# A second PSUM bank for every other head pair's weighted sums in the first batch, with a redrawn order of work

## The chip, the cores and the metric

The kernel runs on one core of a Trainium2 chip. The metric is the device time of one execution in microseconds (us). The core has five engines that run side by side: TensorE (PE, matrix products, with its weight loads PEld), VectorE (DVE), ScalarE (ACT), GpSimd (POOL) and SyncE (SP, which here only issues DMAs). Results of matrix products go to PSUM, an accumulator memory of eight banks.

## What is computed

Attention over the best key chunks, followed by a two-layer MLP with an ELU between its layers. There are 4 batches, 8 heads, 768 positions and 64 dimensions per head. For every query, an upper bound of its score with each chunk of 32 keys is worked out from the minimum and maximum of the chunk's keys; the six best chunks are kept.

```python
ub = np.sum(np.maximum(q[:, :, :, None, :] * k_min[:, :, None, :, :],
                       q[:, :, :, None, :] * k_max[:, :, None, :, :]), axis=-1)
ub = np.where(causal, ub, -1000000000.0)
top_chunks = np.argsort(ub, axis=-1)[..., -top_k:]
...
scores = np.where(mask, scores, -1000000000.0)
attn = np.exp(scores - np.max(scores, axis=-1, keepdims=True))
attn = attn / (np.sum(attn, axis=-1, keepdims=True) + 1e-09)
x = np.matmul(attn, v)            # then heads side by side: 3072 x 512
h = x @ w_in                      # 512 x 2048
g = np.where(h > 0.0, h, np.exp(np.minimum(h, 0.0)) - 1.0)
out = g @ w_out                   # 2048 x 512
```

## The kernel before

**Tiles and stages.** The queries are cut into nine blocks. Batch 0 has three blocks of 256 positions (blocks 0, 1 and 2), every later batch two of 384. Heads go in pairs, four pairs (j = 0 to 3) to a block. For each block i:

- *loads*: k, q and v of 128 positions at a time (L463), into buffers kld, qld and vld. Block 0's k and q are loaded by SP and ACT, most of blocks 1 and 2 by POOL's queue. The weights w_in (L480) and w_out (L484) come as four pieces each on POOL's queue. `SW_ORDER` fixes the order in that queue: k1, v0, q1, v1, the four pieces of w_in, k2, q2, v2, the four of w_out.
- *prep_k, prep_q*: PE transposes k and q (L501) into PSUM; VectorE takes chunk maxima and minima (L521), ScalarE copies out (L528, L533, L548, L553), VectorE makes the positive part of q (L564).
- *select*: PE works out the bounds (L586), VectorE transposes them (L597), takes the best eight (L604), compares (L608) and transposes the masks back (L614 for blocks 0 to 2).
- *score*: PE makes the scores of a pair (L649, with a causal mask added by L652 in blocks 0 and 1), ScalarE the exponentials into pt (L668).
- *weigh*: PE makes the weighted sums and, in a 65th column per head, the sum of the weights (L703). VectorE takes the reciprocal (L712) and multiplies (L714) into the tile on. In the first and the last block PE transposes on (L722) and VectorE copies it into xt (L725); elsewhere a DMA transposes it (L727).
- *mlp*: h = x @ w_in on PE (L744), the exponential on ScalarE (L748), a step on POOL (L750), maximum and minimum on VectorE (L752), then g @ w_out on PE (L765), a copy on ScalarE (L769) and the store (L772).

**PSUM.** Seven banks form the shared pool psM, from which transposes, bounds, scores and MLP tiles are taken in turn. The eighth is a single fixed tile, `o_bank`: the weighted sums of every head pair go to its columns 0 to 389 (0 to 259 are used by a block of 256). Its columns 400 to 511 take filler matmuls.

**The order of work.** The program does not run its stages one after the other. Every step is handed to a planner (`Plan.op`) with its engine, an assumed time, what it reads and writes, and a priority. The priority is the slot of its block plus an offset from the table `SHIFTS`, which has one number for each kind of step, engine and block. `Plan.run` then plays the engines forward: of the steps whose operands and buffers are ready it takes the one that can start first, and of two that can start at the same time the one with the lower priority number. `EARLY` is the time up to which it assumes shorter latencies: 1100 ns rather than `DMA_END` = 1500 from a DMA's end of transfer to its landing, and 50 rather than `MARGIN` = 80 ns for a dependency between engines. The order that comes out is the program's order on each engine; on the chip each engine follows it strictly and waits on semaphores.

**Fillers.** Where the plan leaves PE idle for longer than about 600 ns before 70 us, the program puts matmuls on constant data into the gap (L886), and 30 of them at the start. They write `o_bank`, and so are ordered against VectorE's reading of that bank.

```python
o_bank = psum["psO"].tile([P, 512], F32, name="o_bank")
...
o3 = Buf("psO", lambda: o_bank[:, 0:6 * (D + 1)].rearrange("p (h q d) -> p h q d", h=2, q=3))
...
            if o.start < FILL_END:
                for _ in range(int((o.start - pe - 100) / FILL_NS) if pe else FILL_FIRST):
                    nc.tensor.matmul(o_bank[:, 400:512], lhsT=junk, rhs=junk[:, 0:112], start=True, stop=True)
```

## Time and profile before

| what | value |
|---|---|
| median of six runs | 290.72 us (289.49 to 292.06) |
| the profiled execution | 292.06 us, of which 290.3 us from the first to the last instruction (the span) |
| granted PE clock, mean | 0.986 |
| PE in the span | 275.7 us busy |
| matmuls of the output layer (L765) | 384, 99.6 us busy |
| matmuls of the input layer (L744) | 576, 93.2 us |
| scores (L649) | 312, 59.5 us |
| weighted sums (L703) | 672, 29.6 us |
| fillers (L886) | 43, 5.6 us |
| reciprocals (L712) | 36, 152 to 197 ns each |
| normalisations (L714) | 36, 414 to 558 ns each |
| DMA | 36.22 MB, mean 125 GB/s |

Times run from the start of the span. A line such as L703 is a line of the code above. A row of the timeline gives the start, the length from the first start to the last end, the engine, the line, the operation, what it writes and reads, and how many instructions it merges; in brackets stands how long the engine was idle before it and what ended the wait. Rows can overlap, since matmuls are pipelined. A row of the waits gives who waited for whom, the total in us, how many times, and the longest. The rows of busy tenths cut the span into 40 slices. A row of a table of windows gives the stretch, its length, the busy time of PE, PEld, DVE, ACT and POOL, then the granted clock of PE, the DMA share and GB/s.

### The profile page before, as it was taken

What the parts mean: (1) busy time and instruction counts of PE and PEld (TensorE: products, weight loads), DVE (VectorE), ACT (ScalarE), POOL (GpSimd) and SP (SyncE); (2) the same over time, 40 slices, a digit from 0 to 9 for tenths busy, and PEclk for the clock granted to TensorE, in tenths of its full rate; (3) what the DMA queues carried; (4) which work ended last, traced back from release to release, by engine and by line L of the source; (5) the groups of instructions that cost most, each with busy time, mean ns of one, the idle gap of its engine ahead of it and who ended that gap; (6) DMA issues with size and microseconds to landing.
All of it is one profiled execution on the core that took longest, in us unless ns stands there. A gap on an engine that the chain in (4) does not pass through costs nothing.

```text
span 290.3 us, 7076 instructions
## 1 busy us (share of the span) xinstructions
PE 275.7 (95%) x2519; PEld 179.0 (62%) x2519; DVE 191.5 (66%) x608; ACT 195.2 (67%) x434; POOL 130.5 (45%) x256
## 2 busy tenths in 40 slices
PE   7786989999999999999999999999999999999993
PEld 6474766688587566766646556656765556655541
DVE  8855887957869967759677966623598757525420
ACT  2895565698366799876855548868875397675530
POOL 8669771039167005852158615631581134204600
PEclk9998979999999999999999999999999999999999
DMA  8899997557956223985269526951212310010031
GB/s 188 228 229 205 290 187 120 128 152 163 213 129 159 58 61 73 256 215 129 47 167 248 136 54 152 232 154 55 65 27 66 88 55 3 0 66 8 0 111 73
DMA packets 86883, 36.22 MB, mean 125 GB/s; under 512 B 74176, under 2 KB 82880, under 8 KB 86848
## 3 DMA queue, kind: packets, MB, share of 16 engines
q1 hardware_dynamic: 79424, 27.38, 39.7%
q0 software_dynamic: 5344, 7.87, 13.3%
q10 hardware_dynamic: 2080, 0.52, 0.8%
q8 instruction: 20, 0.33, 0.5%
q14 instruction: 15, 0.12, 0.2%
HBM read 27.26 MB, written 6.29 MB: 116 GB/s over the span
## 4 chain that ended last, share of the span: by engine, by line
PE 75%; DVE 10%; DMA 7%; ACT 4%; SPq 2%; issue 1%; POOL 0%; ACTq 0%; POOLq 0%
PE psM L765 25%; PE psM L744 23%; PE psM L649 11%; PE o_bank L703 6%; PE psM L501 6%; DMA qld<-in_q_dram 3%; PE psM L586 3%; SPq L463 2%; DVE rhs L614 2%; DMA kld<-in_k_dram 2%; DVE gT L752 2%; DMA xt<-on 1%; DVE kmx L521 1%; ACT pt L668 1%; DVE kst L521 1%
## 5 line engine op out<-in xcount | busy, mean ns | idle before, releaser
L750 POOL TENSOR_SCALAR e<-e 128x384 f32<-128x384 f32 (+1 forms) x120 | 63.4, 535 | 89.7 <-ACT e L748 63.9
L765 PE MATMUL psM<-w_out_sb,gT 128*128 128x512 bf16 x384 | 99.6, 379 | 0.0
L668 ACT ACTIVATE pt<-psM 128x384 bf16<-128x384 f32 (+1 forms) x168 | 81.3, 562 | 18.8 <-PE psM L649 17.0
L744 PE MATMUL psM<-xt,w_in_sb 128*128 128x384 bf16 (+1 forms) x576 | 93.2, 311 | 0.6 <-DMA xt<-on 0.6
L752 DVE SCALAR_TENSOR_TENSOR gT<-psM,e 128x384 bf16<-128x384 f32 (+1 forms) x120 | 67.5, 580 | 32.6 <-POOL e L750 25.7
L748 ACT ACTIVATE e<-psM 128x384 f32<-128x384 f32 (+1 forms) x120 | 62.5, 532 | 30.2 <-PE psM L744 28.1
L744 PEld LDWEIGHTS <-w_in_sb 128*128 128x128 bf16 x576 | 55.9, 99 | 29.3 <-issue 2.4
L649 PE MATMUL psM<-rhs,lhs 96*128 96x256 bf16 (+2 forms) x312 | 59.5, 286 | 0.4 <-DVE rhs L614 0.3
L765 PEld LDWEIGHTS <-gT 128*128 128x128 bf16 x384 | 36.0, 97 | 30.6 <-DVE gT L752 0.6
L561 POOL TENSOR_SCALAR rhs<-QTf 64x384 bf16<-64x384 f32 (+1 forms) x56 | 28.6, 510 | 43.5 <-ACT QTf L548 40.1
L649 PEld LDWEIGHTS <-lhs 96*128 96x128 bf16 x312 | 29.3, 100 | 16.9 <-DVE rhs L614 0.6
L703 PEld LDWEIGHTS <-pt 128*128 128x128 bf16 x672 | 27.0, 98 | 8.5 <-issue 1.8
L769 ACT ACTIVATE osb<-psM 128x512 f32<-128x512 f32 x24 | 14.4, 606 | 23.9 <-PE psM L765 15.2
L703 PE MATMUL o_bank<-vext,pt 128*128 128x65 bf16 x672 | 29.6, 194 | 0.2
L521 DVE TENSOR_REDUCE kmx<-psM 128x12 f32<-128x384 f32 (+1 forms) x36 | 17.7, 505 | 9.4 <-PE psM L501 9.2
L548 ACT ACTIVATE QTf<-psM 128x384 f32<-128x384 f32 (+1 forms) x36 | 15.3, 470 | 10.8 <-PE psM L501 10.6
L492 POOL TENSOR_SCALAR vext<-vld 128x384 bf16<-128x384 f32 (+1 forms) x36 | 16.6, 480 | 9.5 <-DMA vld<-in_v_dram 8.6
L681 DVE TENSOR_TENSOR pt<-pt,tri 128x512 bf16<-128x512 bf16 x28 | 12.2, 436 | 11.8 <-ACT pt L668 11.7
L501 PE MATMUL psM<-ident_f,kld 128*128 128x128 f32 x96 | 17.2, 306 | 2.2 <-ACT rhs L553 0.6
L714 DVE TENSOR_TENSOR on<-o_bank,rcp 128x384 bf16<-128x384 f32 (+1 forms) x36 | 18.3, 507 | 0.8
L501 PE MATMUL psM<-ident_f,qld 128*128 128x128 f32 x96 | 16.8, 308 | 2.0 <-ACT rhs L553 0.8
L533 ACT ACTIVATE kb<-psM 128x384 bf16<-128x384 f32 (+1 forms) x28 | 14.1, 504 | 5.9 <-DVE kst L521 4.6
(56 smaller groups left out, 208.9 us busy)
## 6 DMA issues: line engine op xcount, KB each, us to landing
out_dram<-osb SPq DMA_DIRECT2D x24, 256.0 KB, 2.3
kld<-in_k_dram SPq DMA_DIRECT2D x19, 256.0 KB, 4.0
qld<-in_q_dram SPq DMA_DIRECT2D x19, 256.0 KB, 3.5
vld<-in_v_dram SPq DMA_DIRECT2D x18, 256.0 KB, 4.0
lhs<-kb SPq DMA_DIRECT2D x48, 48.0 KB, 1.9
w_in_sb<-in_moe_w_in_dram POOLq DMA_DIRECT2D x4, 512.0 KB, 10.3
w_out_sb<-in_moe_w_out_dram POOLq DMA_DIRECT2D x4, 512.0 KB, 9.4
vld<-in_v_dram POOLq DMA_DIRECT2D x6, 256.0 KB, 5.6
```

Source lines behind the costliest of these rows:

```text
L501: nc.tensor.transpose(ps.get()[:, P * n:P * (n + 1)], xb.get()[:, n, hs, :].rearrange("p h d -> p (h d)"), ident_f)
L521: nc.vector.tensor_reduce(out=out, in_=psk.get()[:, 0:w].rearrange("p (c w) -> p c w", w=CHUNK), axis=AX.X, op=o)
L561: pool_op(110 + pool_ns(w), lambda h=h: nc.gpsimd.tensor_scalar(out=rhs[RH[i]][0:64, h, j, 0:w], in0=qtf.get()[64 * h:64 * h + 64, 0:w], s ...
L649: nc.tensor.matmul(sps.get()[:, o + pc:o + pc + n], lhsT=lhs[s][0:96, hd, P * kb:P * (kb + 1)], rhs=rhs[y][0:96, hd, j, c0 - lo:c0 - lo + ...
L668: op("ACT", act_ns(wtot), 140, lambda pt=pt, sps=sps, hd=hd, wtot=wtot: nc.scalar.activation(out=pt.get()[:, hd, 0:wtot], in_=sps.get()[:, ...
L703: nc.tensor.matmul(o3.get()[:, hd, qi, :], lhsT=pt.get()[:, hd, P * qt + off:P * qt + off + P], rhs=vexts[s][:, kb, hd, :], start=(kb == 0 ...
L714: op("DVE", dve_ns(w), 140, lambda: nc.vector.tensor_tensor(out=on.get()[:, 0:nt, :, :].rearrange("p q h d -> p h q d"), in0=o3.get()[:, : ...
L744: op("PE", 1 + w / 2.4, 200, lambda fc=fc, kk=kk, h_ps=h_ps, o=w * (fc - f0): nc.tensor.matmul(h_ps.get()[:, o:o + w], lhsT=w_in_sb[:, kk, ...
L748: op("ACT", act_ns(m * w), 200, lambda e=e, h_ps=h_ps: nc.scalar.activation(out=e.get()[:, 0:m * w], in_=h_ps.get()[:, 0:m * w], func=AF.E ...
L750: op("POOL", pool_ns(m * w), 72, lambda e=e: nc.gpsimd.tensor_scalar(out=e.get()[:, 0:m * w], in0=e.get()[:, 0:m * w], scalar1=-1.0, scala ...
L752: g = op("DVE", dve_ns(m * w), 130, lambda e=e, h_ps=h_ps, f0=f0: nc.vector.scalar_tensor_tensor(out=gT[f0 // 4].get()[:, f0 % 4:f0 % 4 + ...
L765: op("PE", 216, 200, lambda tt=tt, fc=fc, o_ps=o_ps: nc.tensor.matmul(o_ps.get(), lhsT=gT[fc // 4].get()[:, fc % 4, P * tt:P * (tt + 1)], ...
```

## The change

In blocks 0, 1 and 2 (`O_TWO = 3`), the pairs j = 1 and j = 3 take their weighted sums to a tile from the pool psM; pairs 0 and 2, and all pairs of later blocks, keep `o_bank`. The reciprocal and the normalisation read the tile that was chosen. The number of psM banks stays at seven.

Three assumptions of the planner change: `EARLY` goes from 30 to 16 us, the early DMA latency from 1100 to 800 ns, the early margin from 50 to 40 ns. The whole table `SHIFTS` has new numbers, so that the order on every engine can differ over the whole run. The rows below are the ones that the prediction speaks of; the other rows change in the same way.

```diff
+O_TWO = 3
...
-EARLY = 30e3
+EARLY = 16e3
...
-    ('mlp_in', 'PE'): (2.58869, 0.18485, -0.03717, -4.42605, -1.68403, 0.1887, -0.63691, 0.32029, -2.51407),
+    ('mlp_in', 'PE'): (-2.53111, -2.44679, -2.98032, 0.33104, -2.87733, -0.07855, -1.6966, 0.41874, 6.39981),
...
-    ('mlp_out', 'PE'): (0.24075, 0.17459, 0.14942, -0.16027, 6.11871, 0.1171, 7.22562, 0.28947, -0.95423),
+    ('mlp_out', 'PE'): (-10.79, 2.66429, 7.78478, 3.00852, 0.48571, -0.12355, 2.30605, -1.71352, 7.21788),
...
-    ('score', 'PE'): (0.62726, 0.20683, -0.02773, 0.15303, -0.32678, -2.74631, 0.19235, -0.05167, 0.25745),
+    ('score', 'PE'): (2.99497, 0.39571, 0.05518, 0.69914, -0.09628, -9.67742, -0.07612, -6.04773, -0.26933),
...
-    ('select', 'PE'): (-3.8939, -8.46886, -9.81244, -9.94423, -3.54113, -5.76916, -5.21074, -7.35482, -7.76008),
+    ('select', 'PE'): (5.7063, -2.31403, 0.4375, -3.43262, -4.63267, 2.70558, -0.49943, 0.70776, -0.72468),
...
-    ('weigh', 'PE'): (8.24559, -1.30337, -3.1578, -2.868, -0.84271, -0.35438, -0.13752, 4.33018, -0.6965),
+    ('weigh', 'PE'): (0.16623, -7.89219, -11.11109, -10.94577, -20.56845, -12.32231, -16.82659, -6.87226, -5.74106),
...
-                done.end = clock + (1100 if clock < EARLY else DMA_END)
+                done.end = clock + (800 if clock < EARLY else DMA_END)
...
-                o.end = t + o.occ + o.lat + (50 if t < EARLY else MARGIN)
+                o.end = t + o.occ + o.lat + (40 if t < EARLY else MARGIN)
...
-        o3 = Buf("psO", lambda: o_bank[:, 0:6 * (D + 1)].rearrange("p (h q d) -> p h q d", h=2, q=3))
+        ob = buf("psM", [P, 512], F32) if j % 2 and i < O_TWO else Buf("psO", lambda: o_bank)
+
+        def o3():
+            return ob.get()[:, 0:6 * (D + 1)].rearrange("p (h q d) -> p h q d", h=2, q=3)
...
-                nc.tensor.matmul(o3.get()[:, hd, qi, :], lhsT=pt.get()[:, hd, P * qt + off:P * qt + off + P],
+                nc.tensor.matmul(o3()[:, hd, qi, :], lhsT=pt.get()[:, hd, P * qt + off:P * qt + off + P],
                                  rhs=vexts[s][:, kb, hd, :], start=(kb == 0), stop=(kb == qt))
...
-        op("DVE", 100, 120, lambda: nc.vector.reciprocal(out=rcp.get()[:, :, 0:nt], in_=o3.get()[:, :, 0:nt, D:D + 1]),
-           reads=[o3], writes=[rcp])
+        op("DVE", 100, 120, lambda: nc.vector.reciprocal(out=rcp.get()[:, :, 0:nt], in_=o3()[:, :, 0:nt, D:D + 1]),
+           reads=[ob], writes=[rcp])
```

## Prediction

> **What bounds the kernel now.** I read the page's engine rows first, then the waits of PE, then the timeline of PE over the head, and last tables of windows there.
>
> ```profile
> PE 275.7 (95%) x2519; PEld 179.0 (62%) x2519; DVE 191.5 (66%) x608; ACT 195.2 (67%) x434; POOL 130.5 (45%) x256
> PE   7786989999999999999999999999999999999993
> ...
> PE o_bank L886 <- DVE on L714: 3.0, 4, 0.8
> ```
>
> PE is the bound: 14.6 us of the span are not PE. Of these about 1.1 lie before the first instruction, 4.7 after the last matmul (285.57 of 290.3), 7.4 between 4 and 40 us, and only about 1.4 anywhere between 40 and 285 us. So an order of work can gain next to nothing after 40 us; it can lose there. The largest single wait of PE is a filler matmul (L886) that waits for VectorE's normalisation L714 to let go of the output bank: 4 times 0.75 us. The timeline of PE shows where:
>
> ```profile
> 20.86 0.22 PE L703 MATMUL o_bank<-vext,pt 128*128 128x65 bf16 x2
> 21.82 0.21 PE L886 MATMUL o_bank<-junk 128*128 128x112 bf16 x1 [0.73 <-DVE on L714]
> 21.87 0.27 PE L722 MATMUL psM<-ident_b,on 128*128 128x128 bf16 x2
> 21.98 0.34 PE L703 MATMUL o_bank<-vext,pt 128*128 128x65 bf16 x6
> 23.07 0.21 PE L886 MATMUL o_bank<-junk 128*128 128x112 bf16 x1 [0.75 <-DVE on L714]
> 23.12 0.27 PE L722 MATMUL psM<-ident_b,on 128*128 128x128 bf16 x2
> 23.23 0.35 PE L703 MATMUL o_bank<-vext,pt 128*128 128x65 bf16 x6
> ```
>
> Reader: this is block 0, one head pair after another: weighted sum (L703), VectorE, transposes (L722), next pair. One pair takes 1.25 us (21.82 to 23.07), and PE works about 0.5 of it. It goes on until 25.79, where the first MLP (L744) begins. The third view, busy time in windows of 3.4 us, shows a second price:
>
> ```profile
> 22.90:26.30 3.40, 1.72 (x26) 1.33 (x26) 2.10 (x9) 2.28 (x8) 3.40 (x6) 1.00 1.24 206
> 26.30:29.70 3.40, 3.40 (x22) 2.08 (x29) 1.35 (x5) 1.04 (x2) 3.09 (x4) 0.50 1.25 209
> ...
> 36.50:39.90 3.40, 2.24 (x15) 1.21 (x13) 3.28 (x9) 2.34 (x7) 2.49 (x6) 1.00 1.21 195
> 39.90:43.30 3.40, 3.39 (x28) 3.02 (x29) 2.84 (x7) 2.28 (x7) 3.00 (x8) 0.51 1.19 177
> ```
>
> The columns are length, busy PE, PEld, DVE, ACT, POOL, then the granted clock. After a window with 1.72 us of PE work, the next ran at 0.50; after one with 2.24 us, again 0.51. Each such stretch costs 3.4 x 0.5 = 1.7 us of full-speed work. The six runs support that size: 289.49, 289.93, 289.97 in one group and 291.47, 291.61, 292.06 in another, 1.9 us apart, about one stretch. The profiled execution is the 292.06 one, span 290.3 and 1.76 around it.
>
> **What the Trainium skill says.** "TensorE: Matmul & The Clock Gate", section "What's actually happening": PE's clock is halved after a window of about 3.4 us that was too idle and restored after a busy one, and the window runs freely. The two stretches agree in length (3.4 us); the place of the window against the program I take as a matter of luck. "PSUM — Partial Sum Buffer", section "PSUM bank collisions raise a hardware error": two engines must be kept apart by bank, not by address. The trace agrees: the filler writes columns 400 to 511, the normalisation reads columns up to 259, and the filler still waits 0.75 us. "PSUM", section "Engine vs sequencer instructions": matmuls start in program order. So everything behind a waiting matmul waits too; the transposes after each filler show it.
>
> **The change, part by part.**
> *The bank.* In blocks 0 to 2, pairs 1 and 3 write their weighted sums to one of the seven psM banks. In block 0 the sums of pair j+1 can then run while VectorE normalises pair j. What is late next is VectorE itself: its reciprocal 0.10 (busy after overlap, 0.17 as listed), normalisation 0.43, copy L725 0.29, gaps of 0.02 to 0.04, so about 0.85 per pair in place of 1.25. Four pairs: 4 x 0.40 = 1.6 us. In the blocks 1 and 2, PE has scores and MLP between the sums (41 to 60 us, idle 0.1 us): gain 0.
> *Pool pressure.* Each of the six pairs holds one of seven psM banks from the first sum to the end of the normalisation, about 0.9 us (0.3 + 0.55). Six times 0.9 over 7 banks is 0.8 us at most if the pool were what PE waits for. The waits of PE after 45 us name no bank (only two DMAs, 0.6 and 0.5), so I take 0, with 0.8 as the upper end; a gain below nothing is excluded, since the pool does not grow.
> *The new priorities.* Each number of SHIFTS moves a group of one engine and block in the planner's order, with no new work. For block 0 the sums on PE go from 8.25 to 0.17, the scores from 0.63 to 2.99: sums used to come behind the scores of all four pairs, and now come as soon as a pair's exponentials are there. VectorE sat idle 2.18 us before 21.12, so the chain can start earlier, up to 1.5 us (first sums near 19.5 in place of 20.46 to 20.9, masks of L614 end at 18.9). But two things hold the end. ScalarE finishes its last exponential of block 0 at about 21.8; with sums 0.3, reciprocal and normalisation 0.55, transposes 0.2 and copy 0.3 that gives 23.2. And w_in: its four loads issue at 16.5 to 18.7 on POOL and land 7.6 to 13.0 us later, so not before 24.1; v of block 1 and the casts of v of block 0 stand ahead of them in the same queue. So the MLP of block 0 starts at 24.1 at best, 25.79 now: 1.7 us for bank and order together, which I take (bounds: 0.7, if only half the overlap is planned; 1.7).
> *What follows.* The select of block 1 (L586 at 29.4) heads a VectorE chain from 30.7 to 38 that holds PE at 34.8 and 39.2 (0.31 and 0.65 us; a third wait, 0.45 at 37.6, is for ScalarE). It moves up with the MLP. It could move further: its q is copied by 24.6, so L586 could run near 25.5 rather than 29.4. Value between 0 and about 2 us (the 1.4 us of stalls and 0.6 of filler time); I take 0.3.
> *The clock.* A denser 20 to 26 us may spare the first stretch, and a different 36 to 40 us the second: 0 to 3.4 us in the profiled execution, minus 1.7 if a new one appears. The median of before already holds half of one such event. I take half a stretch, 0.85 us, less the slack below.
> *Planner constants.* EARLY from 30 to 16 us, 1100 to 800 and 50 to 40: these are times that the planner assumes, no instruction changes. For 16 to 30 us it now assumes later DMA landings, so PE is handed fewer operands too soon. Taken at 0; bounds are the stalls of the head.
> *After 40 us.* 1.4 us of idle PE can only shrink by that; a redrawn order of 56 loads and 28 transposes on SP's queue can open new waits like the 0.62 us one for xt at 145.9. Taken at +0.3, bounds -1 and +4.
>
> Sum: -1.7 - 0.3 - 0.85 + 0.3 = -2.55 us. Against the profiled 292.06 this gives 289.5; the median lies 1.34 lower because half of its runs show the cheaper head, so 290.72 - 2.55 = 288.2 us.
>
> **Rivals.**
> *A, the forecast*, 288.2 us, own range 286.6 to 289.2.
> *B, the whole head is repacked.* For it: all 7.4 us of idle and 3.4 us of half clock lie before 44 us, and VectorE is idle from 18.9 to 21.1 and from 27.4 to 29.4. Against it: DMA is full from 16 to 46 us (shares above 1). Bank and order 1.7, both stretches 3.4 less the half event (0.85) in the median, stalls of select 1.2: 290.72 - 5.45 = 285.3 us.
> *C, hidden.* The gain of block 0 is swallowed at the next gate (w_in, or VectorE's masks of block 1, which pin 34.8 us): 0.7 left, spent on one new wait of about 0.6 us: 290.6, range 289.3 to 292.1.
> *D, slower: PE stands before w_out.* The out-MLP of block 0 goes from 0.24 to -10.79 on PE, so it comes first as soon as the planner thinks w_out is in SBUF. On the chip w_out is issued at 30.5 to 36.2 and lands 7.7 to 13.1 us later, 38.2 to 49.3; before, its first matmul runs at 44.8 and waits for nothing. If the plan puts it 3 us too early, scores and transposes behind it stand 3 us, and the idle window brings a half-clock stretch of 1.7: +4.7 - 1.7 = +3.0, so 293.7. It decides once the wait for w_out exceeds the 1.7 us that the bank gains. For it: the shift is the largest of the table's PE rows in block 0, and DMA is full there. Against: the order is made with modelled transfers, and no matmul waited for w_out before.
> That the bank is not used as said I exclude: the test on j and i selects six of the 36 pairs outright.
>
> **Numbers.** A 0.38, B 0.14, C 0.19, D 0.29. A and B are faster: 0.52. C is within 0.5% (1.45 us, about what a measurement of this kernel can tell from no change): 0.19. D is slower: 0.29. The range runs from 284.8 (a little of B below) to 293.7 (about half of D above), which leaves out less than 2 in 10; A's own range is 286.6 to 289.2.
>
> **What would show it.** Right: L886 no longer waits for L714; sums of a pair run before the transposes of the pair ahead; L744 starts at 24 to 24.8 us; the granted clock at 26 us is 1.0 in most executions. Wrong: L744 as late as 25.8, or a wait of PE at L765 for w_out, or idle PE of over 2 us after 45 us, or new windows at half clock.

## The result, and the profile after

The changed kernel takes 292.3 us in the median of 33 runs (290.12 to 296.16); the kernel before, run beside it, 290.44 us in 70 runs (288.13 to 292.89). The ratio is 1.0063, with a 95% interval of 1.0045 to 1.0081. So the change made the kernel 0.6% slower, 1.9 us, where 2.5 us less had been forecast; the time moved the other way, but lies inside the stated range. The profiled execution has a span of 290.2 us.

The engine row and PE's row of slices from the page of the kernel after, to be held against those of before:

```profile
PE 275.1 (95%) x2516; PEld 177.7 (61%) x2516; DVE 196.4 (68%) x608; ACT 193.7 (67%) x434; POOL 129.8 (45%) x256
PE   6697799899999999999999999999999999999994
```

By these PE is as busy as it was (275.7 us before), and nothing here shows where 1.9 us went. Line numbers after are those of before plus 1 up to the scores (L650) and plus 5 from the sums on (L708, L749, L770).

The timeline of PE over the head of the kernel after:

```profile
20.83 0.49 PE L708 MATMUL o_bank<-vext,pt 128*128 128x65 bf16 x6
...
21.45 0.34 PE L708 MATMUL psM<-vext,pt 128*128 128x65 bf16 x6
...
22.06 0.28 PE L727 MATMUL psM<-ident_b,on 128*128 128x128 bf16 x2
22.18 0.35 PE L708 MATMUL o_bank<-vext,pt 128*128 128x65 bf16 x6
...
24.20 0.28 PE L727 MATMUL psM<-ident_b,on 128*128 128x128 bf16 x2 [0.51 <-DVE on L719]
```

This is what the change was to do. The sums of pair 1 run into a psM bank (21.45) before the transposes of pair 0 (22.06), and the four waits of 0.75 us on a filler are gone; one of 0.51 is left. The largest waits of PE in the whole kernel after are these (us in total, times, the longest):

```profile
PE psM L650 <- DVE rhs L615: 2.6, 2, 1.9
PE psM L502 <- ACT rhs L554: 2.5, 3, 1.8
PE psM L749 <- DMA w_in_sb<-in_moe_w_in_dram: 1.2, 2, 0.6
```

The first one stands right behind the head, where the scores of block 1 wait for their masks (before, 0.31 us at that place, but behind a stretch at half clock; 1.22 us in E11 below, which has before's order on PE and no such stretch). It looks like the culprit, and the experiments show that it is not. The loss is in a place where this list shows almost nothing. In the windows of busy time the columns are length, then busy time and number of PE, PEld, DVE, ACT and POOL, the granted clock, the share of the DMA engines and GB/s. The kernel before:

```profile
64.00:68.00 4.00, 4.00 (x39) 3.57 (x38) 1.89 (x3) 3.39 (x8) 3.57 (x7) 1.00 0.44 97
68.00:72.00 4.00, 4.00 (x37) 3.34 (x35) 2.79 (x6) 3.76 (x9) 3.83 (x8) 1.00 0.81 186
```

The kernel after:

```profile
64.00:68.00 4.00, 4.00 (x39) 3.63 (x37) 3.13 (x5) 2.84 (x5) 3.00 (x5) 1.00 0.57 128
68.00:72.00 4.00, 3.73 (x30) 2.55 (x27) 2.91 (x6) 4.00 (x11) 3.17 (x7) 1.00 1.02 270
```

Read the second row of each. PE's "busy" column falls from 4.00 to 3.73 us, ACT is the engine without a pause, and PE makes 30 matmuls in place of 37 and 27 weight loads in place of 35. The busy column hides most of the loss, because the ends of matmuls are modelled and a row of short matmuls with pauses between looks nearly full. But the counts do not size it either. E11, which has the order of before on PE and runs at full clock there, has in the same window

```profile
68.00:72.00 4.00, 4.00 (x30) 2.55 (x28) 3.51 (x10) 3.44 (x8) 3.47 (x7) 1.00 1.13 257
```

that is, as few matmuls and as little PEld as the kernel after: 12 of its matmuls are long ones with w_out. What tells them apart is the duration of each matmul, added up (the next part says how): 4.0 us of work in this window in before and in E11, 2.8 us in after. "Perfetto Trace Analysis" of the Trainium skill, section "Identifying the Most-Contended Engine", says that the busy share of matmuls is a poor measure, and that the work done as a share of what the window could hold at peak and the busy share of weight loads are to be read instead. For the matmuls' busy share this table agrees (4.00 and 3.73 for 4.0 and 2.8 us of work); the weight loads would have misled here (2.55 us in E11 and in after). The timeline of PE there, kernel before:

```profile
67.22 0.38 PE L649 MATMUL psM<-rhs,lhs 96*128 96x256 bf16 x2
67.44 1.04 PE L744 MATMUL psM<-xt,w_in_sb 128*128 128x256 bf16 x8
68.31 0.50 PE L649 MATMUL psM<-rhs,lhs 96*128 96x256 bf16 x4
68.64 1.91 PE L744 MATMUL psM<-xt,w_in_sb 128*128 128x256 bf16 x16
70.39 0.60 PE L649 MATMUL psM<-rhs,lhs 96*128 96x256 bf16 x4
```

and kernel after:

```profile
67.90 0.60 PE L650 MATMUL psM<-rhs,lhs 96*128 96x256 bf16 x4
68.34 0.49 PE L502 MATMUL psM<-ident_f,kld 128*128 128x128 f32 x3
68.75 1.19 PE L650 MATMUL psM<-rhs,lhs 96*128 96x256 bf16 x8
70.05 0.55 PE L502 MATMUL psM<-ident_f,qld 128*128 128x128 f32 x3
70.44 0.60 PE L650 MATMUL psM<-rhs,lhs 96*128 96x256 bf16 x4
```

Before, the scores of block 2 come two or four at a time between MLP products of block 1. After, the products are through earlier and the scores stand next to each other, with only the short transposes of block 3's k and q between. ScalarE in the kernel after, same place:

```profile
68.89 2.37 ACT L669 ACTIVATE pt<-psM 128x512 bf16<-128x512 f32 x5
71.06 0.58 ACT L549 ACTIVATE QTf<-psM 128x384 f32<-128x384 f32 x1
71.43 1.68 ACT L669 ACTIVATE pt<-psM 128x512 bf16<-128x512 f32 x3
```

An exponential takes 2.37/5 = 0.47 us for 512 columns, that is for two scores of 256, which PE makes in 0.22 us. In such a row PE goes at ScalarE's pace (ACT is busy for 4.00 of the 4 us), and hardly a pause is long enough for the list of waits.

**TensorE's work counted out.** To find such a loss I gave each matmul its duration back to back at full clock as the traces show it (0.216 us for an out product of 512 columns, 0.162 and 0.109 for an MLP-in product of 384 and 256, 0.109 for an f32 transpose, 0.029 for a weighted sum) and added up in program order; a record that a trace misses is filled in from the order. The sum is 254.2 us in every kernel here. The table says at what time how much of it was done. Before and after are the profiled executions; E11 and E9 are runs below whose orders on PE are those of before and after and whose granted clock is 1.0 in the record from 20 us to the last product, so from there on they compare without the clock. Each row is one execution:

```
work done (us)       18      34      42      50      58      82     234 
before            42.89   59.92   68.13   76.34   84.41  109.18  264.93
after             41.64   59.60   67.72   77.64   85.72  110.05  265.55
E11 (as before)   40.79   57.58   65.79   74.01   82.07  106.85  262.70
E9  (as after)    39.84   57.79   65.92   75.84   84.10  109.42  264.92
```

At 40 us the order of after leads by 0.95 us (39.84 against 40.79). At 34 us of work it is 0.2 behind, at 50 it is 1.8 behind, and it stays 1.8 to 2.6 behind up to the last product. From 18 to 50 us of work the order of before takes 33.2 us and that of after 36.0: 2.8 us lost. About 0.9 of it falls near 48 to 58 us (the scores of block 2 follow each other there too, with one wait of 0.68 us for their masks), 1.7 near 66 to 76. Behind the last product the kernel after is the shorter one (4.43 us from its start to the end of the span in E9, 5.14 in E11), so the spans of the two executions, 289.6 and 288.1 us, are 1.5 apart and not 2.2.

### The profile page after: what moved, and what is told of

Same layout as the page of the kernel before. It is cut to its first block, busy times and chain, and to the rows that moved or that the text cites. A ratio compares the mean times of both kernels' runs of the same rounds, so it can differ in the third digit from the quotient of the medians.

```text
span 290.2 us, 7069 instructions
## 1 busy us (share of the span) xinstructions
PE 275.1 (95%) x2516; PEld 177.7 (61%) x2516; DVE 196.4 (68%) x608; ACT 193.7 (67%) x434; POOL 129.8 (45%) x256
## 4 chain that ended last, share of the span: by engine, by line
PE 82%; DMA 5%; DVE 4%; POOL 4%; ACT 2%; issue 1%; ACTq 0%; POOLq 0%
PE psM L770 28%; PE psM L749 26%; PE psM L650 12%; PE o_bank L708 6%; PE psM L502 6%; DMA vld<-in_v_dram 4%; PE psM L587 3%; DMA kld<-in_k_dram 1%; DVE gT L757 1%; POOL vext L493 1%; POOL kld L464 1%; POOL vld L464 1%; DVE rhs L615 1%; ACT pt L669 1%; DVE thr L605 1%
## 5 line engine op out<-in xcount | busy, mean ns | idle before, releaser
L770 PE MATMUL psM<-w_out_sb,gT 128*128 128x512 bf16 x384 | 101.8, 379 | 0.0
L749 PE MATMUL psM<-xt,w_in_sb 128*128 128x384 bf16 (+1 forms) x576 | 94.7, 311 | 1.2 <-DMA w_in_sb<-in_moe_w_in_dram 1.2
L669 ACT ACTIVATE pt<-psM 128x384 bf16<-128x384 f32 (+1 forms) x168 | 82.6, 608 | 17.2 <-PE psM L650 15.1
L749 PEld LDWEIGHTS <-w_in_sb 128*128 128x128 bf16 x576 | 55.5, 99 | 28.5 <-DMA w_in_sb<-in_moe_w_in_dram 1.6
L650 PE MATMUL psM<-rhs,lhs 96*128 96x384 bf16 (+2 forms) x312 | 59.2, 287 | 3.0 <-DVE rhs L615 2.6
L770 PEld LDWEIGHTS <-gT 128*128 128x128 bf16 x384 | 36.6, 97 | 33.3 <-issue 1.7
L650 PEld LDWEIGHTS <-lhs 96*128 96x128 bf16 x312 | 29.5, 100 | 20.4 <-issue 2.2
L708 PEld LDWEIGHTS <-pt 128*128 128x128 bf16 x672 | 26.3, 98 | 6.9 <-DVE pt L682 0.9
L708 PE MATMUL o_bank<-vext,pt 128*128 128x65 bf16 x588 | 24.9, 194 | 0.0
L549 ACT ACTIVATE QTf<-psM 128x384 f32<-128x384 f32 (+1 forms) x36 | 15.9, 470 | 5.2 <-PE psM L502 4.9
L522 DVE TENSOR_REDUCE kst<-psM 128x12 f32<-128x384 f32 (+1 forms) x36 | 17.6, 501 | 0.9 <-PE psM L587 0.9
L502 PE MATMUL psM<-ident_f,kld 128*128 128x128 f32 x96 | 16.1, 289 | 1.2 <-ACT rhs L554 0.7
```

What stands on the lines that cost most here:

```text
L502: nc.tensor.transpose(ps.get()[:, P * n:P * (n + 1)], xb.get()[:, n, hs, :].rearrange("p h d -> p (h d)"), ident_f)
L522: nc.vector.tensor_reduce(out=out, in_=psk.get()[:, 0:w].rearrange("p (c w) -> p c w", w=CHUNK), axis=AX.X, op=o)
L650: nc.tensor.matmul(sps.get()[:, o + pc:o + pc + n], lhsT=lhs[s][0:96, hd, P * kb:P * (kb + 1)], rhs=rhs[y][0:96, hd, j, c0 - lo:c0 - lo + ...
L669: op("ACT", act_ns(wtot), 140, lambda pt=pt, sps=sps, hd=hd, wtot=wtot: nc.scalar.activation(out=pt.get()[:, hd, 0:wtot], in_=sps.get()[:, ...
L708: nc.tensor.matmul(o3()[:, hd, qi, :], lhsT=pt.get()[:, hd, P * qt + off:P * qt + off + P], rhs=vexts[s][:, kb, hd, :], start=(kb == 0), s ...
L749: op("PE", 1 + w / 2.4, 200, lambda fc=fc, kk=kk, h_ps=h_ps, o=w * (fc - f0): nc.tensor.matmul(h_ps.get()[:, o:o + w], lhsT=w_in_sb[:, kk, ...
```

## The experiments

Each kernel runs five rounds beside the kernel before. The edits reorder operations after the plan is made: `group(engine, stage, block)` is the list of a stage's operations in planned order, `ahead(engine, ops, first)` moves them ahead of another on that engine's queue, everything else stays. Number of fillers and operations are those of the kernel that is edited unless said. The ratio is what the comparison of the runs gives, not the quotient of two medians. The last column is the time from 18 to 50 us of TensorE's work in the profiled execution (36.0 after, 33.2 before at full clock). What E10 has over 36.0 goes with a stretch at half clock (38.9 to 45.7 us).

```
                                    median  n   ratio to before, 95%        18 to 50
E1  after, w_in products first      292.66  22  1.0068 [1.0042, 1.0093]     36.0
E2  after, comparisons first        292.5   22  1.0063 [1.0036, 1.0089]     36.0
E3  after, one bank                 292.19  18  1.0063 [1.0032, 1.0095]     35.8
E4  before, two banks in block 0    290.11  14  0.9974 [0.9943, 1.0005]     33.2
E5  after, scores mixed into MLP-in 293.93   6  1.0101 [1.0045, 1.0157]     35.4
E6  after, MLP-out mixed in         292.47  22  1.006  [1.003,  1.009]      36.0
E7  E1 + E5 + E6                    292.47  22  1.0067 [1.0039, 1.0096]     35.2
E8  before, MLP-in bundled          291.85  22  1.0038 [1.0008, 1.0068]     33.6
E9  after, two loads early          293.08  11  1.0078 [1.0045, 1.0112]     36.0
E10 E9 + E1                         292.48  22  1.0069 [1.0043, 1.0095]     37.2
E11 before, one load late           290.19  22  0.9999 [0.9974, 1.0024]     33.2
E12 E4 + loads early                290.63  14  1.0002 [0.9976, 1.0028]     33.2
E13 after, 44-80 us as before       295.43   6  1.019  [1.0156, 1.0225]     34.1
E14 before, 44-80 us as after       299.5    6  1.0314 [1.0273, 1.0356]     37.2
E15 after to 44 us, then before     292.11   8  1.0055 [1.0017, 1.0092]     34.1
E16 after, 32-106 us as before      290.44  22  1.0009 [0.9984, 1.0034]     33.2
E17 before, 34-108 us as after      291.5   22  1.0046 [1.0022, 1.007]      36.0
E18 after to 32 us, then before     290.0   22  0.9983 [0.9959, 1.0008]     33.2
```

### E1 to E4: is it the head?

E1 takes away the wait for masks at 34.4 us by placing products ahead of the waiting scores; E2 moves the two comparisons of the mask chain (L609) ahead of an ELU step on VectorE; E3 keeps the order of after and sends every sum to the one bank, where it waits for the normalisation of the pair ahead; E4 keeps the order of before and gives block 0 the second bank, with its sums ahead of the transposes and the four fillers there dropped.

```diff
@@ E1
+    ahead("PE", group("PE", "mlp_in", 0)[48:], group("PE", "score", 1)[0])
@@ E2
+    late = [o for o in group("DVE", "mlp_in", 0)][2]
+    sel1 = group("DVE", "select", 1)
+    selb_ops = sel1[5:7]
+    ahead("DVE", selb_ops, late)
@@ E3
-        ob = buf("psM", [P, 512], F32) if j % 2 and i < O_TWO else Buf("psO", lambda: o_bank)
+        ob = Buf("psM", lambda: o_bank) if j % 2 and i < O_TWO else Buf("psO", lambda: o_bank)
@@ E4
+        two = j % 2 and i == 0
...
+    for j in range(3):
+        ahead("PE", [o for o in pe if getattr(o, "sums", None) == j + 1], turns[j])
+    for j in range(3):
+        ahead("DVE", norms[j + 1][:2], norms[j][2])
```

> The changed kernel with one edit in PE's order: the 16 products of block 0 with the last piece of w_in stand ahead of the first scores of block 1, not behind them. Theory O (the redrawn order costs the time: PE stands 1.95 us at 32.5 to 34.4 for the masks of block 1 while 16 ready products, 1.8 us at full clock, lie behind): the stall at the first scores falls to below 0.4 us and the time falls by 1.0 to 2.5 us, to 290 to 291. Theory P (the second bank costs, through the pool): no change, 292.3 within 0.5. Theory C (only the place of the half-clock stretches differs): no change in the median.

> The changed kernel with one edit in VectorE's order: the two comparisons of block 1's select stand ahead of the ELU step before them. In the changed kernel these two take 1102 and 689 ns (about 240 each before) and end 0.15 us after three ELU steps of POOL. Theory O with the lock (VectorE and POOL exclude each other there): both comparisons start about 0.6 us earlier, at least the first takes below 400 ns, the masks come 1 to 1.7 us earlier and the stall of PE at the first scores of block 1 shrinks from 1.95 to below 1 us; time lower by 0.5 to 1.7 us. If the lock is not the cause, the two keep their length and only 0.6 us is gained. Theory P or C: no change in time.

> The changed kernel with all weighted sums in the one output bank again; the order of every engine is kept, so sums of a pair now wait for the normalisation of the pair ahead. Theory O (the bank itself helps a little, up to the arrival of w_in): block 0's first MLP product starts at 25.8 to 26.2 us in place of 25.12, time higher by 0 to 0.8 us, 292.3 to 293.1. Theory P (the bank costs): time lower by 0.5 us or more. Theory C: no change.

> The kernel before, its order kept, with only block 0 changed: pairs 1 and 3 sum into a psM bank, each pair's sums stand ahead of the transposes of the pair ahead of it, VectorE's reciprocal and normalisation likewise, and the four fillers between are left out. The bank alone, without the redrawn order. Theory O: first MLP product at about 24.4 to 24.8 us (held by w_in) in place of 25.79, time lower by 0.5 to 1.3 us, 289.1 to 289.9. Theory P: time the same or higher. Rival H (the gain is hidden by the masks of block 1, which hold PE at 34.8 in any case): first MLP product earlier, but the first scores of block 1 where they were, time within 0.3 us.

E1, E2 and E3 leave the median where the kernel after has it. In E1 PE no longer waits for the masks, but the scores then wait for ScalarE and the next ELU steps (0.40, 0.24, 0.87 us), and 18 us of work are done at 40.1, no earlier than in E9, where PE does stand 1.95 us. E2 did not even shorten the wait, which stayed at 2.00 us: with the comparisons first, they still took 1.79 us together. E2, VectorE and then GpSimd:

```profile
31.27 1.79 DVE L609 TENSOR_TENSOR selb<-ubT,thr 128x128 bf16<-128x128 f32 x2
```

```profile
31.63 1.90 POOL L755 TENSOR_SCALAR e<-e 128x512 f32<-128x512 f32 x3
```

In the kernel before the same two take 0.48 us, between two steps of GpSimd (33.04 to 33.66, and from 33.92 on):

```profile
33.75 0.48 DVE L608 TENSOR_TENSOR selb<-ubT,thr 128x128 bf16<-128x128 f32 x2
```

"SBUF — State Buffer" of the Trainium skill, section "SBUF: two separate sides", says that a VectorE operation with two SBUF inputs and a GpSimd operation that reads SBUF exclude each other for the whole instruction; the two timelines agree with it (1.79 against 0.48).

E3 says that the bank by itself is worth nothing that can be measured in the order of after, though block 0's first MLP product starts at 25.31 us in it and at 24.49 in E9. E4 says that in the order of before it is worth 0.26% by the ratio, with an interval that just holds none. E4's profile shows where the gain goes. Its first MLP product starts at 24.23 us, 1.3 us earlier than the 25.51 of E11, and then the scores of block 1 wait for their masks and start no earlier. E4, then E11:

```profile
34.00 0.50 PE L649 MATMUL psM<-rhs,lhs 96*128 96x256 bf16 x3 [1.70 <-DVE rhs L614]
```

```profile
33.81 0.50 PE L649 MATMUL psM<-rhs,lhs 96*128 96x256 bf16 x3 [1.22 <-DVE rhs L614]
```

None of the four explains a loss. E1 and E2 do not clear the head by themselves, since neither gave PE its time back by 40 us. The counted work does (a lead of 0.95 us there), and so does E18 below, which has the head of after up to 32 us and loses nothing that can be measured.

### E5 to E8: is it scores without products between?

E5 mixes the last scores of block 2 into the MLP-in products of block 1, on PE and ScalarE alike; E6 puts four of the last MLP-out products of block 0 ahead of the waiting scores of block 2; E7 is E1, E5 and E6 together; E8 does the reverse to the kernel before and puts the last 24 MLP-in products of block 1 ahead of the scores between them, with the same move on ScalarE.

```diff
@@ E5: for e in PE and ACT; m: mlp_in of block 1 in eight steps of n; s: the last scores of block 2
+        ahead(e, s[0:1], m[5 * n])
+        ahead(e, s[1:3], m[6 * n])
+        ahead(e, s[3:5], m[7 * n])
@@ E6: after: scores of block 2 that stand ahead of last
+    last = group("PE", "mlp_out", 0)[24:]
+    ahead("PE", last[0:4], after[2])
@@ E8: s: scores of block 2 between products 32 and 63 of m, the mlp_in of block 1
+    ahead("PE", m[40:], s[0])
+    a, x = group("ACT", "mlp_in", 1), group("ACT", "score", 2)
+    ahead("ACT", a[5:], x[-9])
```

> The changed kernel with one edit on PE and ScalarE: the products of block 1's input MLP, which the changed order runs as one piece (62.3 to 67.4 us) ahead of the scores of block 2, are mixed with five of these scores and their exponentials, as the kernel before mixes them. Theory M (the redrawn order spends its MLP products early, so that at 68 to 76 us PE has only scores and transposes, which ScalarE bounds at 0.5 to 0.6 us per exponential): time lower by 0.7 to 1.5 us than the changed kernel, 290.8 to 291.6, and more matmuls start between 68 and 72 us than the 30 of the changed kernel. Rival (the time is lost elsewhere, or in the clock alone): 292.3 within 0.5.

> The changed kernel with one edit in PE's order: of the last eight products of block 0's first two output tiles (55.2 us), four stand ahead of the scores that PE waits for at 53.3 to 54.0 us. Theory M: PE's wait for the masks of block 2 (0.68 us) is filled, time lower by 0.3 to 0.9 us, 291.4 to 292.0. Rival: no change, because the chain of masks, scores and exponentials behind it ends where it did; 292.3 within 0.4.

> The changed kernel with three edits: the last w_in piece of block 0 ahead of the scores of block 1, both kinds of mixing of MLP products with scores from the two runs beside this one. Theory M with the head: what the head gains is kept now, 289.8 to 290.8 us, level with the kernel before. Rival: still above 291.8.

> The kernel before with the opposite edit: the last 24 products of block 1's input MLP stand ahead of the scores of block 2 with which they are mixed, on PE and ScalarE. Theory M: slower by 0.7 to 1.5 us than the kernel before, fewer matmuls between 68 and 72 us than its 37. Rival: no change within 0.4 us.

E8 says that bundling does cost something (1.0038, interval above 1), of which its profile shows 0.4 us in the counted stretch. But mixing products in by hand did not win it back. The counted work says why: E7 needs 0.8 us less than the kernel after from 18 to 50 us of work, and 1.2 us more from 50 to 66 (17.4 against 16.2). The scores of block 3 come up earlier there and stand before masks that are not in yet. E7, PE:

```profile
83.48 0.83 PE L650 MATMUL psM<-rhs,lhs 96*128 96x384 bf16 x6 [0.87 <-DMA rhs<-msk]
```

The loss had moved, not gone. I took this for a sign that the theory was wrong, and looked elsewhere first.

### E9 to E12: is it late loads?

Several runs of the order of after showed a wait in the middle that others did not. E2 again, PE and SyncE's queue:

```profile
108.90 0.66 PE L502 MATMUL psM<-ident_f,kld 128*128 128x128 f32 x4 [1.46 <-DMA kld<-in_k_dram]
```

```profile
97.59 4.98 SPq L625 DMA_DIRECT2D rhs<-msk  x8
102.67 1.20 SPq L732 DMA_TRANSPOSE xt<-on  x1
103.92 0.58 SPq L464 DMA_DIRECT2D kld<-in_k_dram  x1
```

The third k load of block 5 stands behind eight mask transfers and lands 4.9 us after its issue, when PE is already there. E9 moves it ahead of the masks and the third q load of block 5 to its siblings; E10 adds E1; E11 puts the same k load four issues later in the kernel before; E12 is E4 with the loads of least slack issued earlier.

```diff
@@ E9: k5, q5, k6, v5: loads of blocks 5 and 6 on SP
+    ahead("SP", k5[2:], group("SP", "select", 4)[0])
+    ahead("SP", q5[2:], seqs["SP"][seqs["SP"].index(q5[1]) + 1])
@@ E11
+    ahead("SP", k5[2:], seqs["SP"][seqs["SP"].index(k5[2]) + 4])
@@ E12
+    k6[0].deps = [d for d in k6[0].deps if d not in v5]
+    ahead("SP", q5, group("SP", "prep_k", 5)[0])
+    ahead("SP", k6, v5[0])
```

> The kernel after with two DMA issues moved on SyncE's queue and nothing else: the third k load of block 5 goes ahead of the eight mask transfers of block 4 (it stood behind them, was issued at 103 to 105 us and landed 0 to 1 us before TensorE's transposes of it, or after them), and the third q load of block 5 goes next to its two siblings (issued at 116, 0 to 1.6 us of slack). Theory late loads (L): the redrawn order of the queue made these two loads late, and the runs of the kernel after mostly lose 0.5 to 1.5 us there. Then no wait of TensorE for kld or qld shows between 100 and 122 us, and the median falls from 292.3 by 0.5 to 1.5 us, to 290.8 to 291.8. Rival (absorbed, A): those waits only take up time that TensorE or ScalarE would lose further on; the waits go and the median stays within 0.4 us of 292.3. Rival (moved, M): the masks, now 0.6 us later in the queue, or the next loads become the late ones, with waits of the same sum and no gain.

> The kernel after with the two loads early as in the run before it and with block 0's last w_in products ahead of block 1's first scores (the edit that alone left the median at 292.66). Theory L: the head's gain of about 1.5 us was eaten by the loads, which have a fixed place in SyncE's queue and do not come earlier when TensorE does; with both, the median is 1.0 to 2.5 us below 292.3, 289.8 to 291.3. Rival A: both edits are absorbed later, the median stays at 292 to 292.6.

> The kernel before with one DMA issue moved: the third k load of block 5, which has 1.2 us of slack, goes four issues later on SyncE's queue (behind three copies of k and a weighted-sum transpose), 2 to 3 us later. Theory L: TensorE waits 1 to 2.5 us for it near 96 us, and the median rises by 0.7 to 2 us over that of the kernel before, 290.4 to 291.1 to 292.4: a late load of this kind alone is then worth the whole difference between the two kernels. Rival A: the wait shows but the median rises by under 0.4 us.

> The kernel before with the bank of the change in block 0 (sums ahead of the transposes, four fillers dropped; alone 290.11, ratio 0.9974) and with the loads that had least slack issued earlier: the three q loads of block 5 ahead of the copies of block 5's k, the three k loads of block 6 ahead of the v loads of block 5. Theory L: the wait of 0.84 us for kld at 126 us goes and the head's gain arrives: 288.5 to 289.7 against 290.4 of the kernel before, the first to beat both. Rival A: 289.9 to 290.5, no different from the bank alone. Rival M: the v loads of block 5, now three issues later, make the weighted sums of block 5 wait and the median rises over 290.5.

The theory fell with E9, which gains nothing though the wait near 109 us is gone in its profile. E11 decides nothing: its median did not rise, but in its profile PE waits for no k load anywhere from 85 to 110 us, so the load only used up its slack and was not late. Late loads cost PE up to 1.46 us in single executions (E2 above); that they make the difference between the two kernels is what E9 speaks against. E10 and E12 add nothing either: E10 is as slow as E1, and E12 is level with the kernel before. E9 and E11 also gave complete traces at full clock, and these made the table of counted work above: the loss is made between 40 and 76 us.

### E13 to E15: the stretch exchanged, with bad seams

The two kernels have the same 2837 planned operations, so their orders can be joined in a list ORDER: all operations that one plan starts before a time, then the rest in the other's order. E13 is the kernel after with the operations of 44 to 80 us of the plan in before's order, E14 the reverse, E15 the kernel after to 44 us with before's order behind. Where an order with the one bank follows, the second bank is used only in the blocks that need it.

```diff
-    plan.run()
...
+    by = {o.id: o for o in plan.ops}
+    plan.order = [by[x] for x in ORDER]
```

> The kernel after with its own order up to 44 us of the plan and again behind it, but the 350 operations that the kernel before starts up to 80 us (all five engines' queues) in the order of before. PE's work counted out from the traces of the two kernels at full clock says that the kernel after is 0.95 us ahead when 18 us of TensorE's work are done (at 40 us), 1.8 us behind when 50 us are done (at 76 us), and 1.7 to 2.3 us behind from there to the end. Theory bunching (B): the whole loss of 2.8 us is made between 44 and 80 us, where the redrawn order puts scores of block 2 next to each other (4, 5 and 3 in a row, where before has one or two between MLP products), so that TensorE runs at ScalarE's pace; with before's order there the median falls by 2 to 3 us, to 289.3 to 290.3. Rival (whole body, W): the loss only shows there first, and is made again in the rest of the redrawn order, as after the three edits that mixed products in: 291.5 to 292.5. Rival late loads: 291.5 or more as well, with waits for kld at 105 to 110 us.

> The kernel before in its own order, but the 390 operations from 44 to 80 us of the plan in the order of the kernel after (with a second bank for the weighted sums of the pairs there, as in the kernel after). Theory B: this stretch alone makes the loss: 290.5 + 2 to 2.8 = 292.4 to 293.3, slower than the kernel before by 0.6 to 1.0%. Rival W: the loss needs the rest of the redrawn order too, and this one is within 0.8 us of 290.5.

> The first 420 operations (up to 44 us of the plan) in the order of the kernel after with the second bank in block 0, everything behind them in the order of the kernel before. Theory B: the head's lead of about 0.95 us is kept because nothing behind it takes it: 289.3 to 289.8 against 290.5, ratio 0.996 to 0.998. Rival (absorbed, A): the lead is used up by waits in the order of before too, as in the kernel before with the bank alone (0.9974, interval 0.9943 to 1.0005): 290.1 to 290.6.

E13 won back 1.9 us inside the stretch (34.1 against 36.0), and lost 5.4 us behind its second seam, from 50 to 66 us of work (21.8 against 16.4 in before's order), where the two orders have not done the same operations. About 3.4 of the 5.4 are the clock: 6.8 us ran at half of it there. E13, PE at the seam (L800 is the scores' line in the joined kernels), and the window behind it:

```profile
83.97 1.31 PE L800 MATMUL psM<-rhs,lhs 96*128 96x384 bf16 x9 [1.60 <-DMA rhs<-msk]
85.54 2.93 PE L800 MATMUL psM<-rhs,lhs 96*128 96x384 bf16 x13 [0.27 <-issue]
```

```profile
85.40:92.20 6.80, 6.66 (x59) 3.08 (x59) 4.18 (x13) 5.43 (x12) 1.03 (x2) 0.50 0.44 98
```

Scores of block 3 wait for masks, and then thirteen follow each other. E14 lost about 4 us in the same part of its work, at full clock. All three missed their numbers, and none decides between the theories.

### E16 to E18: the same with clean seams

At 32 us of after's plan and 34 of before's, the done sets differ by one operation; at 108 and 106.5 by 18. E16 is the kernel after with before's order between these seams, E17 the mirror, E18 the kernel after up to the first seam and before's order from there on.

> As the mid run before it, with the seams where the two orders have done the same operations: the first 284 operations (32 us of the plan) of the kernel after with the second bank in block 0, then the 813 that the kernel before starts up to 106 us in before's order, then the rest of the kernel after. The run with seams at 44 and 80 us won back 1.9 of the 2.8 us inside the stretch and lost 5.4 us right behind its second seam, where mask transfers and their selection were late. Theory B (the loss is made between 40 and 76 us): 289.3 to 290.3, 2 to 3 us below the kernel after. Rival W (the rest of the redrawn order loses as much): 291.5 or more. If it stays above 291.5, TensorE's work counted out shows whether the loss stands at the seam or is spread.

> The mirror: the kernel before, with one output bank in block 0, up to 34 us of its plan, then the 822 operations that the kernel after starts up to 108 us in its order (with its second bank in blocks 1 and 2), then the rest of the kernel before. Theory B: the stretch alone costs 1.9 to 2.8 us, 292.3 to 293.2 against 290.4, at full clock 50 us of TensorE's work done at 76 to 77 us instead of 74. Rival W: within 0.8 us of 290.4.

> The first 284 operations (32 us of the plan) in the order of the kernel after with the second bank in block 0, everything behind them in the order of the kernel before. Theory B: the head's gain up to there, 0.5 us by TensorE's work counted out (10 us of it done at 28.14 instead of 28.70 us), is kept: 289.7 to 290.1, ratio 0.997 to 0.999. Rival A (absorbed): 290.2 to 290.6, ratio 1.0.

E16 is at 1.0009 [0.9984, 1.0034], against 1.0063 [1.0045, 1.0081] for the kernel after: with that one stretch in the old order the loss is no longer measurable. (Its median, 290.44, lies 0.14 above the range expected, and 1.1 below where the rival begins.) E17 is at 1.0046 [1.0022, 1.007]: the new order in that stretch alone makes the kernel before slower. (Its median, 291.5, lies under the 292.3 expected and above the rival's 291.2; by the ratios about three quarters of the loss came with the stretch.) Both exchange the banks of blocks 1 and 2 together with the order; E3, which has the order of after with one bank and is as slow as after, says that the banks are not what counts. The counted work repeats to 0.1 us: 33.2 in E16, 36.0 in E17. The windows in E17:

```profile
64.00:68.00 4.00, 3.90 (x36) 3.16 (x33) 3.34 (x6) 3.45 (x8) 2.90 (x6) 1.00 1.05 274
68.00:72.00 4.00, 3.61 (x24) 2.37 (x25) 3.08 (x9) 4.00 (x11) 3.41 (x8) 1.00 0.92 212
```

and in E16:

```profile
64.00:68.00 4.00, 4.00 (x40) 3.59 (x38) 2.80 (x5) 3.39 (x7) 3.83 (x7) 1.00 0.50 113
68.00:72.00 4.00, 3.95 (x30) 2.87 (x30) 3.16 (x7) 3.65 (x9) 3.84 (x8) 1.00 1.06 242
```

By the added durations PE does 6.2 us of work in these 8 us in E17 and 8.0 in E16; in E17 ScalarE is full from 68 to 72. E18 has the lowest median of the eighteen, 290.0 against 290.93 of the kernel before beside it, but its interval holds 1. The head's gain is at most 0.4%, and no version measurably beats the kernel before.

What stays open: which of the operations in that stretch have to move. The order asks ScalarE and VectorE for more before 58 us of PE's work (138 and 223 instructions, 58.4 and 67.3 us of their busy time in E9; 130 and 214, 55.2 and 60.8 in E11), which fits that relief in one place moved the loss to the next (E5, E7). That this front load is the reason, and how much of the loss the rows of scores make, is argued from these sums; that the order of the stretch makes the loss is shown. Behind 106 us the order of after may cost a further few tenths (E16 over E18 is 0.26%, with overlapping intervals).

## Why the prediction was wrong

- *The bank: right in mechanism, and nearly in size.* Sums run ahead of the transposes, and the filler's four waits are gone. From one reciprocal of VectorE to the next a pair takes 0.56, 0.75 and 0.83 us (they start at 21.36, 21.92, 22.67, 23.50), where 0.85 was reckoned. The bank alone (E4) brings the first MLP product 1.3 us forward, where 1.6 were reckoned. "Pool pressure" at 0 is not contradicted: E3, which takes no bank from the pool for sums, is no faster than the kernel after.
- *"I take 1.7" for bank and order together: too much.* The MLP of block 0 starts at 25.12, 0.67 us earlier and not 1.7; that is the lower bound given. At full clock it is 1.0 us (24.49 in E9, 25.51 in E11). The reason named was the right one: w_in. PE waits for it twice, 0.59 us each, and in E18 the first wait is 1.73 us. The upper value had been taken from the earliest landing of one piece.
- *Rival C had the next gate right.* It said that the gain could be swallowed by VectorE's masks of block 1, and in E4 it is: 1.3 us ahead at the MLP, 0.2 behind at the scores of block 1. C did not foresee a loss (290.6 us, at most 292.1).
- *The select of block 1, -0.3: right in sign only over the whole head.* PE stands 1.95 us for its masks (1.22 in E11 at full clock), since the 16 products that could fill the time stand behind the scores. Still the lead at 18 us of work is 0.95 us at full clock, bank, order and select together, where 2.0 had been summed. E18 has 0.17% of it in its ratio, 0.5 us, not clear of nothing.
- *The clock, -0.85: not refuted, and thinly shown.* Of the runs of the kernel before beside the experiments, 215 of 250 have a mean granted clock below 0.997, of those of the kernel after 24 of 34 (the profiled one among them). The others have a mean of 289.4 us before (35 runs) and 292.0 after (10 runs), 2.6 us apart, and the medians are 1.9 apart. Taken at face value, the change gave back about 0.7 us by fewer stretches at half clock; but the runs come from several sessions, and the record leaves out the first microseconds (see the end).
- *"After 40 us ... Taken at +0.3, bounds -1 and +4": this is the step that failed.* In its place the runs show +2.8 us between 40 and 76 us (E9 against E11; E16 and E17 show that the order of this stretch makes it). The bound held it; the value did not, for two reasons. First, "about 1.4 us idle between 40 and 285 us" was read from busy columns with modelled ends, which show a row of scores at ScalarE's pace as work. Counted out, the 216 us of work from 18 to 234 take 221.9 us in E11, so even the order of before loses 5.9 us there and not 1.4, and neither figure says how much another order can lose. Second, the risk was placed on SP's queue (loads and transposes). Late loads do occur, and E9, which takes two of them away, gains nothing. The queue that mattered in the two places seen is PE's own: how many MLP products the plan leaves between scores. The table of SHIFTS was in the diff, with the score, weigh and mlp_out rows of blocks 0 to 2 moved, and I read it only for block 0.
- *Rival D, slower, had the right sign and the wrong mechanism.* The first MLP-out product ran at 44.94 without a wait for w_out; before it ran at 44.8.

In sum, at full clock and by one execution of each order: -0.95 for the head, +2.8 for the stretch, +0.4 from there to the last product and -0.7 behind it make +1.5, where -1.7 without the clock had been summed. The measured difference of the medians is +1.9, and of the means of runs at full clock 2.6. Executions of one kernel differ by as much as these figures do among themselves (290.12 to 296.16 after), so the rest is not settled.

## What to carry to other kernels

When a change redraws a whole plan, its named part can be the smaller term, as here (0.95 us gained in the head, 2.8 lost behind it). Compare what stands next to what on the bounding engine, stage by stage, and add up the full-speed durations of its matmuls per window: a busy share of 93% hid that 2.8 us of work were done in 4, and counts of matmuls did not tell it either. Where the consumer of scores (0.47 us on ScalarE for two) is slower than they are (0.22 us), look at whether products of another stage stand between them; taking them out cost time (E8), putting some back by hand moved the loss (E5, E7). To find where an order loses, exchange one stretch of it for the old one, with seams where both have done the same operations; seams elsewhere cost more (about 4 us in E14) than the effect looked for.

## What the hardware showed that I had not expected

- One order has different clocks in its head. The profiled execution of the kernel after stood at half clock from 7.5 to 21.1 us and again from 34.8 to 38.2, behind PE's stand for the masks; E9, with the same order on PE and the same stand of 1.95 us, had no half clock there. Two traces are not to be compared over a head like this before the clock is taken out. The kernel after:

```profile
7.50:21.10 13.60, 10.75 (x89) 8.05 (x88) 8.89 (x39) 11.92 (x36) 9.86 (x15) 0.50 0.90 226
31.40:34.80 3.40, 1.46 (x15) 1.12 (x13) 3.34 (x9) 1.19 (x2) 3.36 (x6) 1.00 1.04 329
34.80:38.20 3.40, 3.40 (x22) 2.60 (x20) 3.23 (x8) 2.13 (x5) 1.18 (x2) 0.50 1.17 214
```

and E9:

```profile
31.40:34.80 3.40, 1.45 (x17) 1.14 (x15) 3.29 (x7) 1.33 (x4) 3.40 (x6) 1.00 1.06 327
34.80:38.20 3.40, 2.88 (x29) 2.44 (x26) 3.28 (x8) 2.71 (x7) 1.16 (x2) 1.00 1.17 209
```

- The column of the granted clock says 1.00 where there is no record yet. E9's record begins at 19.8 us and the column gives 1.00 before it, but PE went at half pace there: eight f32 transposes at 4.80 us take 2.16 us, and 0.212 us from one to the next, against 0.109 later. The record of the kernel after begins at 4.1 us, with full clock up to 7.5, and the same eight take 1.39 us. So a mean clock of 1.0 does not say that the whole head ran at full speed. E9, then the kernel after:

```profile
4.80 2.16 PE L502 MATMUL psM<-ident_f,kld 128*128 128x128 f32 x8 [0.72 <-DMA kld<-in_k_dram]
```

```profile
4.48 1.39 PE L502 MATMUL psM<-ident_f,kld 128*128 128x128 f32 x8 [0.40 <-DMA kld<-in_k_dram]
```

- Under load, a k load of 128 positions landed 3.1 us after its issue in E1's profile and 4.9 us in E2's, on the same place of the queue. By these figures a load that has 1 us of slack in one execution can be late in the next.
